# Pairs of heads, value products turned round, and the feed-forward part dealt out between score tiles: a rewrite of a hash-attention kernel

## The chip, the cores and the metric

The kernel runs on one core of one Trainium2 chip. The metric is the device time of one execution in microseconds (us); lower is better. A core has a matmul engine (PE, with a separate record PEld for loading its weights), a vector engine (DVE), an engine for activation functions (ACT), a general one (POOL), and queues that issue transfers (DMA). A matmul holds one operand still in the array, the weights or stationary operand, and streams the other past it column by column. In these kernels its results land in PSUM, a memory whose parts are called banks, and DVE and ACT read them there and write theirs to SBUF, where the operands lie. The "granted clock" is the share of full speed at which PE's clock ran, as the profile records it.

Times quoted are medians of several executions. The jobs ran on several chips; the old kernel's median was between 422.7 and 424.2 us in all of them. A run is labelled slow when it lies more than 1.5% above the fastest of the same kernel.

## The reference, cut to what matters

```python
# q, k, v: (4, 8, 768, 64); proj: (64, 6)
q_bits = (einsum('bhsd,dk->bhsk', q, proj) > 0)      # six sign bits for each token
k_bits = (einsum('bhsd,dk->bhsk', k, proj) > 0)
mask   = q_bucket[..., :, None] == k_bucket[..., None, :]
scores = where(mask, q @ k.T / sqrt(64), -1e9)
attn   = softmax(scores)                             # a tiny constant is added to the sum
x      = (attn @ v).transpose(0, 2, 1, 3).reshape(3072, 512)
h = x @ w_in                                         # layer 1: 512 -> 2048
return (h * cos(h)) @ w_out                          # layer 2: 2048 -> 512
```

Both kernels get the mask without a masking step: they append the six bits as ±constants to the 64 columns of q and k, so that a score is much larger where all six agree, and a bias in the exp brings every other score down to zero. The bits need fp32, because a product near zero must have the right sign. That is "the hash".

## The kernel before

It takes one head after the other, and starts the feed-forward part when all 32 heads are done. For a head, PE transposes q and k in fp32, DVE copies the result out of PSUM, PE does the hash matmul on it, DVE turns the sums into bits:

```python
def emit_prep_a(hd):                                     # L142
    for t in range(SB):                                  # SB = 6
        nc.tensor.matmul(out=psum_t[:, t*P:(t+1)*P], lhsT=qk_nat[:, t, :],
                         rhs=ident, is_transpose=True, ...)
    nc.vector.tensor_copy(out=qk_f32, in_=psum_t)
    ...
def emit_prep_b(hd):                                     # L159
    for c0, c1 in ((0, 512), (512, 768)):
        nc.tensor.matmul(out=psum_t[0:38, c0:c1], lhsT=projx2,
                         rhs=qk_f32[:, c0:c1], start=True, stop=True)
    nc.vector.tensor_scalar(out=q_ext[D:KEXT, :], in0=psum_t[0:NBITS, :], ...)   # bits of q
    nc.vector.tensor_scalar(out=k_ext[D:KEXT, :], in0=psum_t[32:32+NBITS, :], ...)
```

Then six score tiles of 128 keys by 768 queries, an exp of each, and the value products. There V (64 columns, and 64 columns of ones for the denominator) is the stationary operand and the exp tile streams, 768 columns and one more:

```python
out_ps = att_ps.tile([P, 1024], FP32, name="out_ps")     # two banks, one buffer
def emit_attnv(jt):                                      # L210
    for ci, (c0, c1) in enumerate(((0, 512), (512, S + 1))):
        nc.tensor.matmul(out=out_ps[:, c0:c1], lhsT=v_ext[:, jt, :],
                         rhs=pt_sb[:, c0:c1], start=(jt == 0), stop=(jt == SB - 1))
...
nc.vector.tensor_scalar(out=numpair[b][t][r0:r0+D, :], in0=out_ps[0:D, 0:S], ...)
nc.scalar.copy(out=denpair[b][t][r0:r0+D, :], in_=out_ps[D:P, 0:S])   # on ACT
```

When all heads are done, ACT computes 1/den as exp(−ln(den)), DVE multiplies, and six chunks of 512 tokens go through layer 1 and then layer 2.

The softmax here doesn't subtract the row's maximum and nothing guards it: scores larger than these inputs give would overflow.

Of the kernel before, what the change touches and what calls it, by code (L numbers as in the profile page):

```python
# [11 lines left out]
FP16 = mybir.dt.float16  # L12

Q_PRESCALE = 1.0 / 416.0
EXP_SCALE = 52.0
EXP_BIAS = -78.0
# [4 lines left out]
def kernel(  # L21
# [11 lines left out]

# [5 lines left out]
    N_TOK = B * S  # L39
    P = 128  # L40
    SB = S // P
    KEXT = D + NBITS
    NH = B * H
    NFT = D_MODEL // P
    NFF = D_FF // P

    glob = ctx.enter_context(tc.tile_pool(name="glob", bufs=1))

    ident = glob.tile([P, P], FP32)
    make_identity(nc, ident)  # L50

    projx2 = glob.tile([P, 38], FP32)
    nc.vector.memset(projx2, 0.0)
    nc.sync.dma_start(out=projx2[0:D, 0:NBITS], in_=proj)
    nc.sync.dma_start(out=projx2[D:2 * D, 32:32 + NBITS], in_=proj)

    exp_bias = glob.tile([P, 1], FP32)
    nc.vector.memset(exp_bias, EXP_BIAS)
    cos_bias = glob.tile([P, 1], FP32)
    nc.vector.memset(cos_bias, math.pi / 2.0)  # L60

    v_ext_bufs = []
    for i in range(3):
        vt = glob.tile([P, SB, P], FP16, name=f"v_ext{i}")
        nc.vector.memset(vt[:, :, D:P], 1.0)
        v_ext_bufs.append(vt)



    win_t = [glob.tile([P, D_FF], FP16, name=f"win{ft}") for ft in range(NFT)]  # L70
    wout_t = [glob.tile([P, D_MODEL], FP16, name=f"wout{ff}") for ff in range(NFF)]

    xT = [glob.tile([P, N_TOK], FP16, name=f"xT{i}") for i in range(NFT)]

    fence = [glob.tile([P, 1], FP32, name=f"fence{i}") for i in range(4)]

    stage_pool = ctx.enter_context(tc.tile_pool(name="stage", bufs=1))
    numpair = [[stage_pool.tile([P, S], FP32, name=f"num{bb}_{t}") for t in range(NFT)]
               for bb in range(B)]
    denpair = [[stage_pool.tile([P, S], FP32, name=f"den{bb}_{t}") for t in range(NFT)]  # L80
               for bb in range(B)]

    def emit_weight_loads(which):
        if which == 0:
            for ft in range(NFT):
                nc.gpsimd.dma_start(
                    out=win_t[ft], in_=moe_w_in[ft * P:(ft + 1) * P, :]
                )
        else:
            for ff in range(NFF):  # L90
                nc.gpsimd.dma_start(
                    out=wout_t[ff], in_=moe_w_out[ff * P:(ff + 1) * P, :]
                )

    att_stack = ExitStack()
    att_nat = att_stack.enter_context(tc.tile_pool(name="att_nat", bufs=3))
    att_f32 = att_stack.enter_context(tc.tile_pool(name="att_f32", bufs=2))
    att_ops = att_stack.enter_context(tc.tile_pool(name="att_ops", bufs=2))
    att_vs = att_stack.enter_context(tc.tile_pool(name="att_vs", bufs=2))
    att_ptp = att_stack.enter_context(tc.tile_pool(name="att_pt", bufs=1))  # L100
    att_ps = att_stack.enter_context(tc.tile_pool(name="att_ps", bufs=1, space=bass.MemoryType.PSUM))
    att_ps2 = att_stack.enter_context(tc.tile_pool(name="att_ps2", bufs=2, space=bass.MemoryType.PSUM))

    NPT = 6
    pt_bufs = []
    for i in range(NPT):
        ptb = att_ptp.tile([P, S + 8], FP16, name=f"pt_buf{i}")
        nc.vector.memset(ptb[:, S:S + 8], 1.0)
        pt_bufs.append(ptb)

    dma_state = {}
    prep_state = {}

    def emit_dma_v(hd):
        b, h = divmod(hd, H)
        v_ext = v_ext_bufs[hd % 3]
        nc.gpsimd.dma_start(
            out=v_ext[:, :, 0:D],
            in_=v[b, h].rearrange("(t p) d -> p t d", p=P),
        )  # L120

    def emit_dma(hd, k_engine=None, defer_v=False):
        b, h = divmod(hd, H)
        qk_nat = att_nat.tile([P, SB, 2 * D], FP32, name="qk_nat")
        nc.sync.dma_start(
            out=qk_nat[:, :, 0:D],
            in_=q[b, h].rearrange("(t p) d -> p t d", p=P),
        )
        (k_engine or nc.sync).dma_start(
            out=qk_nat[:, :, D:2 * D],  # L130
            in_=k[b, h].rearrange("(t p) d -> p t d", p=P),
        )
        v_ext = v_ext_bufs[hd % 3]
        if not defer_v:
            emit_dma_v(hd)
        dma_state[hd] = (qk_nat, v_ext)

    def emit_prep_a(hd):
        qk_nat, v_ext = dma_state.pop(hd)
        psum_t = att_ps.tile([P, SB * P], FP32, name="psum_t", space=bass.MemoryType.PSUM)  # L140
        for t in range(SB):
            nc.tensor.matmul(  # L142
                out=psum_t[:, t * P:(t + 1) * P],
                lhsT=qk_nat[:, t, :],
                rhs=ident,
                is_transpose=True,
                start=t in (0, 4),
                stop=t in (3, 5),
            )
        qk_f32 = att_f32.tile([P, S], FP32, name="qk_f32")  # L150
        nc.vector.tensor_copy(out=qk_f32, in_=psum_t)
        q_ext = att_ops.tile([KEXT, S], BF16, name="q_ext")
        k_ext = att_ops.tile([KEXT, S], BF16, name="k_ext")
        prep_state[hd] = [psum_t, qk_f32, v_ext, q_ext, k_ext]

    def emit_prep_b(hd):
        psum_t, qk_f32, v_ext, q_ext, k_ext = prep_state[hd]
        for c0, c1 in ((0, 512), (512, 768)):
            nc.tensor.matmul(  # L159
                out=psum_t[0:38, c0:c1],  # L160
                lhsT=projx2,
                rhs=qk_f32[:, c0:c1],
                start=True,
                stop=True,
            )
        nc.vector.tensor_scalar(  # L166
            out=q_ext[D:KEXT, :],
            in0=psum_t[0:NBITS, :],
            scalar1=0.0,
            scalar2=0.5,  # L170
            op0=mybir.AluOpType.is_gt,
            op1=mybir.AluOpType.subtract,
        )
        nc.vector.tensor_scalar(  # L174
            out=k_ext[D:KEXT, :],
            in0=psum_t[32:32 + NBITS, :],
            scalar1=0.0,
            scalar2=0.5,
            op0=mybir.AluOpType.is_gt,
            op1=mybir.AluOpType.subtract,  # L180
        )

    def emit_prep_c(hd):
        psum_t, qk_f32, v_ext, q_ext, k_ext = prep_state[hd]
        nc.vector.tensor_scalar(
            out=q_ext[0:D, :], in0=qk_f32[0:D, :], scalar1=Q_PRESCALE,
            scalar2=None, op0=mybir.AluOpType.mult,
        )
        nc.vector.tensor_copy(out=k_ext[0:D, :], in_=qk_f32[D:2 * D, :])

    emit_dma(0, k_engine=nc.scalar)
    emit_dma(1, k_engine=nc.scalar, defer_v=True)
    emit_prep_a(0)
    emit_prep_c(0)
    emit_prep_b(0)
    emit_dma(2, k_engine=nc.scalar, defer_v=True)
    emit_prep_a(1)
    emit_dma_v(1)

    for hd in range(NH):  # L200
        b, h = divmod(hd, H)
        _psum_t, _qk_f32, v_ext, q_ext, k_ext = prep_state.pop(hd)

        out_ps = att_ps.tile([P, 1024], FP32, name="out_ps", space=bass.MemoryType.PSUM)
        pt_tiles = {}

        def emit_attnv(jt):
            pt_sb = pt_tiles.pop(jt)
            for ci, (c0, c1) in enumerate(((0, 512), (512, S + 1))):
                nc.tensor.matmul(  # L210
                    out=out_ps[:, c0:c1],
                    lhsT=v_ext[:, jt, :],
                    rhs=pt_sb[:, c0:c1],
                    start=(jt == 0),
                    stop=(jt == SB - 1),
                )

        for jt in range(SB):
            st_ps = att_ps2.tile([P, S], FP32, name="st_ps", space=bass.MemoryType.PSUM)
            for c0, c1 in ((0, 512), (512, 768)):  # L220
                nc.tensor.matmul(  # L221
                    out=st_ps[:, c0:c1],
                    lhsT=k_ext[:, jt * P:(jt + 1) * P],
                    rhs=q_ext[:, c0:c1],
                    start=True,
                    stop=True,
                )
            pt_sb = pt_bufs[(hd * SB + jt) % NPT]
            nc.scalar.activation(  # L229
                out=pt_sb[:, 0:S],  # L230
                in_=st_ps,
                func=mybir.ActivationFunctionType.Exp,
                bias=exp_bias,
                scale=EXP_SCALE,
            )
# [13 lines left out]
        if hd + 3 < NH:  # L249
            emit_dma(hd + 3)  # L250
# [175 lines left out]
```

## Time and profile before

| | before |
|---|---|
| time, median of three (range) | 423.73 us (423.16 to 424.43) |
| profiled span, mean granted clock | 420.9 us, 0.983 |
| attention (first exp to last head) | 225.6 us, 7.08 us a head |
| change-over with PE nearly idle | 10.0 us |
| feed-forward part but for its tail | 154.0 us, PE without a gap |

The prediction below shows most of the views that this table is from. Two readings are added here. The first is the timeline of ACT in the middle of attention: start, length, engine, line, operation, result and source, how many; in brackets, the idle time ahead of it and what ended that.

```profile
121.93 0.90 ACT L229 ACTIVATE pt_buf_161<-st_ps,exp_bias 128x768 f16<-128x768 f32 x1 [1.07 <-PE st_ps L221]
122.73 0.89 ACT L229 ACTIVATE pt_buf_163<-st_ps,exp_bias 128x768 f16<-128x768 f32 x1
123.65 0.80 ACT L271 COPY den_3_131<-out_ps 64x768 f32<-64x768 f32 x1
124.47 0.90 ACT L229 ACTIVATE pt_buf_165<-st_ps,exp_bias 128x768 f16<-128x768 f32 x1
```

The COPY is that of the denominator out of `out_ps`. Successive exps start 0.80 us apart though each is recorded at 0.90.

The second is one wait of PE from the list of waits (engine, result, line, whom it waits for: us in total, times, longest).

```profile
PE h_ps L321 <- DVE xT_97 L304: 8.3, 1, 8.3
```

This is the change-over: the first layer-1 matmul waits for the normalised x.

### The profile page before, as it was taken

What the parts mean: (1) busy time and instruction counts of PE and PEld (TensorE: products, weight loads), DVE (VectorE), ACT (ScalarE), POOL (GpSimd) and SP (SyncE); (2) the same over time, 40 slices, a digit from 0 to 9 for tenths busy, and PEclk for the clock granted to TensorE, in tenths of its full rate; (3) what the DMA queues carried; (4) which work ended last, traced back from release to release, by engine and by line L of the source; (5) the groups of instructions that cost most, each with busy time, mean ns of one, the idle gap of its engine ahead of it and who ended that gap; (6) DMA issues with size and microseconds to landing.
All of it is one profiled execution on the core that took longest, in us unless ns stands there. A gap on an engine that the chain in (4) does not pass through costs nothing.

```text
span 420.9 us, 5065 instructions
## 1 busy us (share of the span) xinstructions
PE 384.4 (91%) x1856; PEld 176.4 (42%) x1856; DVE 243.1 (58%) x352; ACT 306.9 (73%) x389; POOL 37.9 (9%) x58
## 2 busy tenths in 40 slices
PE   4889999999999999999999739999999999999996
PEld 1334444444444444444343314444444444444442
DVE  3576676767686768676867337348355372360630
ACT  1478787878787878787878998968788781660831
POOL 6260101010101010111100000000000000000000
PEclk9899999999999999999999959999999999999999
DMA  9999363636363636363611000020020110200202
GB/s 171 206 198 180 62 81 57 83 55 87 52 90 50 93 47 95 48 94 48 93 11 9 0 2 1 0 101 0 0 101 1 51 51 0 101 0 2 100 25 75
DMA packets 81784, 26.54 MB, mean 63 GB/s; under 512 B 76128, under 2 KB 78176, under 8 KB 81760
## 3 DMA queue, kind: packets, MB, share of 16 engines
q1 hardware_dynamic: 51440, 18.29, 18.6%
q0 software_dynamic: 27968, 7.34, 17.1%
q10 hardware_dynamic: 2352, 0.59, 0.7%
q8 instruction: 14, 0.23, 0.2%
q14 instruction: 10, 0.08, 0.1%
HBM read 27.27 MB, written 6.29 MB: 80 GB/s over the span
## 4 chain that ended last, share of the span: by engine, by line
PE 71%; ACT 18%; DVE 5%; issue 4%; DMA 1%; ACTq 0%
PE h_ps L321 20%; PE out_ps L210 10%; PE st_ps L221 9%; PE psum_t L159 8%; ACT pt_buf_167 L229 6%; PE psum_t L142 5%; ACT pt_buf_165 L229 3%; ACT pt_buf_163 L229 3%; ACT pt_buf_161 L229 1%; DMA qk_nat<-in_k_dram 1%; PE o_ps_3374 L353 1%; PE o_ps_3149 L364 1%; PE o_ps_3147 L364 1%; PE o_ps_2925 L364 1%; PE o_ps_2923 L364 1%
## 5 line engine op out<-in xcount | busy, mean ns | idle before, releaser
L337 DVE TENSOR_TENSOR g_sb<-h_ps,cos_sb 128x512 f16<-128x512 f32 x96 | 65.3, 691 | 58.5 <-ACT cos_sb L329 58.3
L221 PE MATMUL st_ps<-q_ext,k_ext 70*128 70x512 bf16 (+1 forms) x384 | 94.2, 328 | 3.6 <-ACT pt_buf_161 L229 1.0
L329 ACT ACTIVATE cos_sb<-h_ps,cos_bias 128x512 f16<-128x512 f32 x96 | 64.8, 692 | 13.9 <-PE h_ps L321 13.4
L221 PEld LDWEIGHTS <-k_ext 70*128 70x128 bf16 x384 | 34.5, 97 | 63.7 <-issue 46.9
L229 ACT ACTIVATE pt_buf_161<-st_ps,exp_bias 128x768 f16<-128x768 f32 x32 | 28.8, 901 | 41.9 <-PE st_ps L221 41.9
L364 PEld LDWEIGHTS <-g_sb 128*128 128x128 f16 x320 | 31.2, 98 | 37.8
L321 PE MATMUL h_ps<-xT_97,win_77 128*128 128x512 f16 x96 | 36.9, 386 | 8.3 <-DVE xT_97 L304 8.3
L142 PE MATMUL psum_t<-ident,qk_nat 128*128 128x128 f32 x192 | 36.5, 277 | 6.8 <-DMA qk_nat<-in_k_dram 4.8
L255 DVE TENSOR_SCALAR vsum_sb<-out_ps 128x1 f32<-128x1 f32 x32 | 5.1, 158 | 62.8 <-PE out_ps L210 62.8
L321 PE MATMUL h_ps<-xT_98,win_78 128*128 128x512 f16 x96 | 36.8, 385 | 0.0
L321 PE MATMUL h_ps<-xT_99,win_79 128*128 128x512 f16 x96 | 36.6, 384 | 0.0
L321 PE MATMUL h_ps<-xT_100,win_80 128*128 128x512 f16 x96 | 36.6, 384 | 0.0
L166 DVE TENSOR_SCALAR q_ext<-psum_t 6x768 bf16<-6x768 f32 x32 | 30.4, 949 | 5.3 <-PE psum_t L159 4.3
L142 PEld LDWEIGHTS psum_t<-ident,qk_nat 128*128 128x128 f32 x192 | 24.1, 142 | 18.5 <-issue 7.6
L229 ACT ACTIVATE pt_buf_165<-st_ps,exp_bias 128x768 f16<-128x768 f32 x32 | 28.8, 901 | 3.4 <-PE st_ps L221 2.7
L229 ACT ACTIVATE pt_buf_167<-st_ps,exp_bias 128x768 f16<-128x768 f32 x32 | 28.8, 901 | 3.1 <-PE st_ps L221 0.7
L174 DVE TENSOR_SCALAR k_ext<-psum_t 6x768 bf16<-6x768 f32 x32 | 30.5, 952 | 0.4
L229 ACT ACTIVATE pt_buf_171<-st_ps,exp_bias 128x768 f16<-128x768 f32 x32 | 28.9, 902 | 0.0
L229 ACT ACTIVATE pt_buf_163<-st_ps,exp_bias 128x768 f16<-128x768 f32 x32 | 28.6, 893 | 0.0
L229 ACT ACTIVATE pt_buf_169<-st_ps,exp_bias 128x768 f16<-128x768 f32 x32 | 28.6, 893 | 0.0
L321 PEld LDWEIGHTS <-win_77 128*128 128x128 f16 x96 | 9.5, 99 | 19.9 <-issue 8.8
L210 PEld LDWEIGHTS <-v_ext_73 128*128 128x128 f16 x132 | 12.8, 97 | 7.7 <-issue 1.7
(721 smaller groups left out, 603.1 us busy)
## 6 DMA issues: line engine op xcount, KB each, us to landing
qk_nat<-in_q_dram SPq DMA_DIRECT2D x32, 192.0 KB, 2.8
out_dram<-o_sb SPq DMA_DIRECT2D x24, 256.0 KB, 2.0
qk_nat<-in_k_dram SPq DMA_DIRECT2D x29, 192.0 KB, 3.9
v_ext_71<-in_v_dram POOLq DMA_DIRECT2D x11, 96.0 KB, 4.6
v_ext_73<-in_v_dram POOLq DMA_DIRECT2D x11, 96.0 KB, 4.3
v_ext_75<-in_v_dram POOLq DMA_DIRECT2D x10, 96.0 KB, 4.3
qk_nat<-in_k_dram ACTq DMA_DIRECT2D x3, 192.0 KB, 4.9
win_77<-in_moe_w_in_dram POOLq DMA_DIRECT2D x1, 512.0 KB, 8.9
```

Of the source, the lines that this page charges most:

```text
L142: nc.tensor.matmul(out=psum_t[:, t * P:(t + 1) * P], lhsT=qk_nat[:, t, :], rhs=ident, is_transpose=True, start=t in (0, 4), stop=t in (3, 5),)
L159: nc.tensor.matmul(out=psum_t[0:38, c0:c1], lhsT=projx2, rhs=qk_f32[:, c0:c1], start=True, stop=True,)
L166: nc.vector.tensor_scalar(out=q_ext[D:KEXT, :], in0=psum_t[0:NBITS, :], scalar1=0.0, scalar2=0.5, op0=mybir.AluOpType.is_gt, op1=mybir.Alu ...
L174: nc.vector.tensor_scalar(out=k_ext[D:KEXT, :], in0=psum_t[32:32 + NBITS, :], scalar1=0.0, scalar2=0.5, op0=mybir.AluOpType.is_gt, op1=myb ...
L210: nc.tensor.matmul(out=out_ps[:, c0:c1], lhsT=v_ext[:, jt, :], rhs=pt_sb[:, c0:c1], start=(jt == 0), stop=(jt == SB - 1),)
L221: nc.tensor.matmul(out=st_ps[:, c0:c1], lhsT=k_ext[:, jt * P:(jt + 1) * P], rhs=q_ext[:, c0:c1], start=True, stop=True,)
L229: nc.scalar.activation(out=pt_sb[:, 0:S], in_=st_ps, func=mybir.ActivationFunctionType.Exp, bias=exp_bias, scale=EXP_SCALE,)
L255: nc.vector.tensor_scalar(out=vsum_sb[:, 0:1], in0=out_ps[:, S:S + 1], scalar1=DELTA, scalar2=None, op0=mybir.AluOpType.mult,)
L321: nc.tensor.matmul(out=h_ps, lhsT=win_t[ft][:, ff * P:(ff + 1) * P], rhs=xT[ft][:, tok0:tok0 + TOK_CHUNK], start=(ft == 0), stop=(ft == NF ...
L329: nc.scalar.activation(out=cos_sb, in_=h_ps, func=mybir.ActivationFunctionType.Sin, bias=cos_bias, scale=1.0,)
L337: nc.vector.tensor_tensor(out=g_sb, in0=h_ps, in1=cos_sb, op=mybir.AluOpType.mult)
L364: nc.tensor.matmul(out=o_ps[tt], lhsT=g_tiles[ff][:, tt * P:(tt + 1) * P], rhs=wout_t[ff], start=(ff == 0), stop=(ff == NFF - 1),)
```

## The change

Its author describes it as "preparation of the first pairs in single steps on units of their own; whole-pair hash at once; value products skipped there and doubled between". Against the kernel before it is a complete rewrite. A "pair" is two heads, a "unit" is one score tile with its exp; there are 192 units. The parts that matter are these, as cut excerpts from both sides.

The value products change their stationary operand. A head's result then needs 396 columns (461 with the small constant in columns of its own), one bank, so two heads can alternate:

```diff
-    for ci, (c0, c1) in enumerate(((0, 512), (512, S + 1))):
-        nc.tensor.matmul(
-            out=out_ps[:, c0:c1],
-            lhsT=v_ext[:, jt, :],
-            rhs=pt_sb[:, c0:c1], ...
+    bank = av_ps[h % 2]
+    for qt in range(T):                                    # T = 6
+        nc.tensor.matmul(
+            out=bank[:, qt * W:qt * W + D + 1],
+            lhsT=pt[:, qt * P:(qt + 1) * P],               # the exp tile is stationary
+            rhs=vx_bufs[pr % 3][:, hh, jt, 0:D + 1], ...   # 65 columns stream
```

The hash of a pair is eight fp32 matmuls of 192 columns. Each of four (q or k, head) goes to 32 columns of the array of its own:

```diff
-    nc.tensor.matmul(out=psum_t[0:38, c0:c1], lhsT=projx2, rhs=qk_f32[:, c0:c1], ...
+    for c in range(2):
+        for j, (w, hh, ts) in enumerate(cols):
+            nc.tensor.matmul(
+                out=hb[32 * j:32 * j + 32, :].rearrange("p (t r) -> p t r", r=32),
+                lhsT=projblk[:, c].rearrange("p b i -> p (b i)"),
+                rhs=blk[pr][w][:, hh, ts[0]:ts[-1] + 1, c, :],
+                start=(c == 0), stop=(c == 1), ...
```

Its input `blk` comes from DVE block transposes. For pairs 0 to 4 small PE matmuls and fp16 PE transposes bring bits and operands into place; for pairs 5 to 15 it is DMA transposes and, for the bits, a DMA. The normalisation is a reciprocal and a multiply on DVE for each head (from the ninth head on after a small copy and an add), and after the start ACT has no copies left. Last, the schedule. Layer 2 of a batch is dealt out among the units of the next, and the steps for pairs 1 to 4 are spread over units, most with one of its own, on which value products are skipped unless more than three units of them are pending:

```diff
+    UF = lambda u: 2 if u % 2==0 else 1        # layer-2 matmuls for a unit
+    ENDF = 6
+    PREP = {1: [0.5, 2, 4.5, 6, 7.5, 9, 9.5, 12, 14], ...}
+    HEAVY = set(int(x) for n in PREP for x in PREP[n][3:]) | set(int(x) for x in SECOND)
...
+        for u in range(U):
+            score(h, jt)
...
+            elif u in HEAVY:
+                avs = len(pend) - MAXP
+            else:
+                avs = min(2, len(pend) - (4 if u < T else LAG))
+            for _ in range(avs):
+                av_step()
...
+            if b > 0:
+                fill(UF(u))                    # layer 2 of the batch before
```

## The prediction

> **What bounds the kernel now.** I read the page first, then the busy time by stage, then the longest pieces of the chain of waits, then single instructions by shape. The page says that the matmul engine is nearly always busy and carries most of the chain; busy is not peak, so the stages have to be told apart.
>
> ```profile
> PE 384.4 (91%) x1856; PEld 176.4 (42%) x1856; DVE 243.1 (58%) x352; ACT 306.9 (73%) x389; POOL 37.9 (9%) x58
> ...
> PE 71%; ACT 18%; DVE 5%; issue 4%; DMA 1%; ACTq 0%
> ```
>
> Busy time in five stretches: up to the first exp, the attention, the change-over, the feed-forward part, its last chunk. The first column after the stretch is its length, then come PE, weight loads, DVE, ACT, POOL, clock, DMA share, GB/s.
>
> ```profile
> 0.00:13.36 13.36, 5.50 (x19) 2.72 (x20) 5.64 (x18) 1.28 (x1) 7.55 (x17) 1.00 1.14 179
> 13.36:239.00 225.64, 209.68 (x1065) 97.77 (x1064) 156.16 (x217) 185.86 (x222) 30.32 (x41) 0.99 0.54 79
> 239.00:249.00 10.00, 1.37 (x8) 0.56 (x7) 2.39 (x5) 9.90 (x12) 0.00 (x0) 0.69 0.00 0
> 249.00:403.00 154.00, 154.00 (x705) 69.25 (x705) 77.59 (x113) 106.78 (x151) 0.00 (x0) 0.99 0.09 35
> ```
>
> The feed-forward stretch has no PE idle time at all; attention is 93% busy; the change-over of 10 us is Ln and Exp on ACT with PE waiting (8.3 us in the chain). Unit prices, from the chain and the groups by shape:
>
> ```profile
> 403.07 3.45 PE o_ps_3371 L353 x16
> ...
> L221 PE MATMUL st_ps<-q_ext,k_ext 70*128 70x512 bf16 x192 | 71.9, 383 | 3.6 <-ACT pt_buf_161 L229 1.0 <-ACT pt_buf_165 L229 0.3 <-ACT pt_buf_163 L229 0.3
> L221 PE MATMUL st_ps<-q_ext,k_ext 70*128 70x256 bf16 x192 | 52.2, 272 | 0.0
> ...
> L142 PE MATMUL psum_t<-ident,qk_nat 128*128 128x128 f32 x192 | 36.5, 277 | 6.8 <-DMA qk_nat<-in_k_dram 4.8 <-issue 2.1
> ```
>
> Sixteen 512-column matmuls take 3.45 us, 0.216 us each, though a single one is recorded at 383 ns: overlap. The 256-column form follows its predecessor by 0.11 us (383 minus 272 ns says the same). So a score tile of 512+256 columns costs 0.325 us of PE. An fp32 hash matmul of 512 columns shows as two records that together last 1.05 us (four passes), and the fp32 transposes start 0.108 us apart. One head takes 7.08 us (its starts are 121.43, 128.51, 135.59), in which streaming is 1.95 scores + 1.95 value products + 1.28 hash + 0.65 transposes = 5.83; the remaining 1.25 us is PE waiting behind the serial chain transposes, DVE copy, hash, DVE bits. Over the kernel: 32 x 1.25 = 40 us of such holes, 13 us start, 8 us change-over, 4 us tail; streaming itself is 62 + 62 + 41 + 21 + 83 + 83 = 352 us.
>
> **What the Trainium skill says.** "TensorE: Matmul & The Clock Gate", section "Back-to-back issue gap": N/2.4 + 2.5 ns for a warm matmul; 0.216 us at 512 columns agrees. The same section gives about 81 ns for 128-column matmuls that each have their own weight load; the old kernel has no small fp16 matmul, so no trace shows it. Its Part 3, "Packing small matmuls", says that matmuls into different 32-column strips run together; not shown yet either. "FP8 and Floating Point Precision", section "TensorE Precision Notes", puts true fp32 at four passes; the 1.05 us above agree. "ScalarE: Activation LUTs", section "Step-by-step: what each stage is for", tells of about 2.7 us for a table load including the drain; here the record is 1.283 us.
>
> **The change part by part.** It is a rewrite. The order of instructions in both builds gives the counts.
>
> 1. Feed-forward arithmetic is the same: layer 1 is 512 matmuls of 384 columns at 0.1625 (estimate from the page's formula), 83.2 us; layer 2 is 384 x 0.216 = 82.9 us. What is new is that layer 2 of one batch is dealt out, one and two matmuls in turn, among the score tiles of the next batch, so that PE has work while ACT does exp.
> 2. Scores: 192 x 0.325 = 62.4 us, unchanged. Exp: 192 x 0.79 (the spacing of successive exps in the timeline) = 152 us of ACT. Exp of batch 0 alone is 56 x 0.79 = 44 us.
> 3. Value products turn round: the exp tile becomes the weight, 65 columns of V stream. 1152 pairs of weight load and matmul replace 384 long matmuls (62.4 us). Price per pair between 0.030 (65/2.4 + 2.5 ns, load hidden) and 0.081 (the page's figure for 128 columns). I choose 0.047: 54 us. This is the largest unknown.
> 4. The 192 fp32 transposes (21 us) go. In their place: DVE 32x32 transposes for the hash, 120 fp16 PE transposes for pairs 0 to 4 (0.07 each, estimate, 8.4 us), DMA transposes for the other eleven pairs.
> 5. Hash: 8 fp32 matmuls of 192 columns per pair, 1536 columns x 4 passes, 2.56 us alone, to four column strips in turn. I take two at a time: 1.5 us a pair, 24 us against 41. Bits of pairs 0 to 4: 24 small matmuls a pair at 0.05 (estimate), 6 us together.
> 6. Normalisation becomes a reciprocal and a multiply on DVE per head; the 32 denominator copies (0.80 us each) and 32 Ln/Exp activations (about 0.85 each) leave ACT, and with them the change-over. x is turned by 16 DMA transposes.
>
> By stage, with 0.325 + 6 x 0.047 = 0.607 per unit: first score at 9 us (13 minus the fp32 hash and transpose of a whole head). Units 0 to 55: 34.0 + four pairs of 4.4 (hash 1.5, bits 1.2, transposes 1.7) + 3.5 for the second half of pair 0 and the delta matmuls = 55 (above ACT's 44). Layer 1 of batch 0: 128 x 0.1625 + one table load 1.3 = 22.1. Batches 1 and 2: 48 x (0.607 + 1.5 x 0.216) = 44.7 + four hashes 6 = 50.7 each, 101.4. Their layer 1 with 16 fills: 25.6 each, 51.2. Batch 3: 40 x 0.931 + 4.5 = 41.7. Left-over value products and layer 2: 4. Layer 1 and 2 of batch 3: 20.8 + 20.7. Last copy and store: 3. Sum 329. The measured time exceeds the profiled span by 2.8 (423.7 against 420.9); 3 more for waits that I did not see: **335 us**. Attention and its change-over give all of it, 249 us to about 165 us of PE time; the feed-forward part gives nothing by itself.
>
> **The rivals.**
> - *The small matmuls cost the page's 81 ns.* 1152 x 0.034 more = 39 us, and some for bits and transposes: 380 us. For it: the weight load, 97 ns in the trace, must be paid somewhere when only 27 ns of streaming hide it. Against: the 97 ns are mostly latency, for loads of 128 fp32 columns hide behind matmuls 0.108 us apart.
> - *The load hides fully and ACT becomes the bound.* At 0.030 the units lose 0.10 us each, some 20 us. A unit is then 0.83 us of PE with its share of hash 0.95, just above exp's 0.79, so ACT limits only batch 0: 317 to 320 us.
> - *The hash does not overlap between strips*: 16 us more, 350. *It overlaps four-wide*: 10 us less.
> - *A new wait*: DVE in batch 0 (copies of 768 fp16 columns out of PSUM, estimate 0.9 us each from the 0.96 us of the old copy, four a pair, plus block transposes) is about 7.5 us of 12 units' 11 us, so close that a late copy stalls a score; POOL now does casts for which no trace has a price; the DMA transposes have five units (about 5 us) to land. Each could add 5 to 15 us, against which speaks that the steps are spread out on units of their own.
>
> **Range and chances.** The price of a small pair moves the sum between 318 and 380, the hash between 325 and 350. I hold 0.03 for about one in three, 0.04 to 0.06 for one in two, 0.08 for one in six. Hence 335, with 313 to 366 eight times in ten. Even with every rival against it the time stays under 415, so slower is left only for a stall I can't see: faster 0.97, within 2% 0.02, slower 0.01.
>
> **What would show it.** Right: no gap of PE over 1 us between the first score and the last tile; line of the value products at 0.04 to 0.06 us start to start; layer 1 at 0.163 and layer 2 at 0.216; exp gaps on ACT in batches 1 to 3, almost none in batch 0; first exp near 9 us; clock 1.0 throughout. Wrong: PE waiting for DVE copies or a DMA transpose at each pair, or value products at 0.08. The prediction fails most likely through the price of the small pairs, next through batch 0.

## The result, and the profile after

| | before | after |
|---|---|---|
| median of four runs of one job (range) | 423.71 us (423.16 to 424.43) | 311.23 us (310.70 to 312.90) |
| ratio (95% interval) | | 0.7356 (0.7333 to 0.7378) |
| profiled span, clock | 420.9 us, 0.983 | 309.5 us, 0.998 |

A ratio here and below is the mean time of one kernel's fast runs over the mean of the other's fast runs in the same rounds, so it is not quite the ratio of the medians. The kernel gained 112.5 us, and 311.23 lies 1.8 us below the predicted range.

The page of the changed kernel: busy time, share of the span and count for each engine, and who carries the chain that ended last.

```profile
PE 299.1 (97%) x3026; PEld 180.2 (58%) x3026; DVE 201.2 (65%) x434; ACT 234.6 (76%) x288; POOL 109.2 (35%) x180
...
PE 79%; ACT 7%; DMA 6%; DVE 4%; issue 2%; POOL 1%; SPq 0%; ACTq 0%; DVEq 0%
```

PE's share rose from 91% to 97% while its busy time fell by 85 us, and ACT's part of the chain fell from 18% to 7%. Next, the busy time in ten stretches of the changed kernel, all but its tail of 3.2 us; the columns are those of the prediction's table (length, PE, weight loads, DVE, ACT, POOL, clock, DMA share, GB/s).

```profile
0.00:8.59 8.59, 6.74 (x65) 2.80 (x66) 3.19 (x14) 2.90 (x6) 3.67 (x18) 1.00 0.67 199
8.59:57.39 48.80, 45.96 (x768) 31.80 (x767) 32.48 (x78) 45.68 (x56) 34.65 (x50) 1.00 0.80 204
57.39:80.20 22.81, 22.68 (x148) 13.59 (x148) 16.55 (x26) 17.88 (x24) 13.27 (x34) 1.00 0.89 164
80.20:124.00 43.80, 42.65 (x507) 26.07 (x506) 35.37 (x88) 39.77 (x48) 27.69 (x39) 1.00 0.77 180
124.00:150.00 26.00, 26.00 (x171) 15.23 (x170) 18.15 (x27) 17.92 (x25) 2.67 (x4) 1.00 0.18 60
150.00:195.00 45.00, 43.75 (x511) 26.45 (x510) 34.70 (x90) 41.02 (x49) 23.97 (x33) 1.00 0.74 164
195.00:221.00 26.00, 26.00 (x171) 15.23 (x170) 17.38 (x26) 17.91 (x24) 0.43 (x1) 1.00 0.04 13
221.00:264.70 43.70, 43.70 (x458) 25.70 (x457) 23.19 (x61) 36.33 (x43) 2.90 (x4) 1.00 0.31 76
264.70:285.50 20.80, 20.80 (x130) 12.53 (x128) 14.26 (x21) 14.29 (x20) 0.00 (x0) 1.00 0.04 13
285.50:306.30 20.80, 20.79 (x113) 10.77 (x110) 5.50 (x8) 0.90 (x1) 0.00 (x0) 1.00 0.19 69
```

In the first stretch with exps (8.59 to 57.39) ACT is busy for 45.7 of 48.8 us: exp is the bound there. In every later one shown PE is, with at most 1.25 us free. These stretches set against the prediction's sum:

| stage | predicted, us | measured, us |
|---|---|---|
| up to the first exp | 9 | 8.6 |
| units 0 to 55 | 55 | 48.8 |
| layer 1 of batch 0 | 22.1 | 22.8 |
| units of batch 1; its layer 1 | 50.7; 25.6 | 43.8; 26.0 |
| units of batch 2; its layer 1 | 50.7; 25.6 | 45.0; 26.0 |
| units of batch 3 and left-overs | 45.7 | 43.7 |
| layer 1, layer 2 of batch 3, tail | 20.8 + 20.7 + 3 | 20.8 + 20.8 + 3.2 |
| sum | 329 | 309.5 |

What one unit looks like, in PE's timeline:

```profile
100.09 0.48 PE L257 MATMUL s_ps<-qx,kx 128*128 128x512 f16 x2
100.41 0.34 PE L283 MATMUL av_ps<-vx,pt 128*128 128x65 f16 x6
100.59 0.59 PE L375 MATMUL m_ps<-wout,g 128*128 128x512 f16 x2
```

From the start of the six value products (100.41) to the start of what follows (100.59) is 0.18 us, 0.03 us for each, although the groups of the same kernel by line (busy us, mean ns of one) say 97 ns for a weight load and 193 for its matmul:

```profile
L283 PEld LDWEIGHTS <-pt 128*128 128x128 f16 x1152 | 56.9, 97 | 19.9 <-issue 0.4
...
L283 PE MATMUL av_ps<-vx,pt 128*128 128x65 f16 x1152 | 64.0, 193 | 0.0
```

Both are latencies that overlap with their neighbours. Only start-to-start spacing is a price. Taken over the whole trace, that spacing is 29 ns for a value pair (median), 0.81 us for the hash of a pair of heads and 0.30 us for a pair's bits (means of pairs 1 to 15 and 1 to 4), and 56 ns for an fp16 transpose (median).

Where PE's time went, as the sum of the intervals from each matmul record to the next, by purpose (a wait is counted to the matmul before it, so the change-over of 8.3 us sits under the value products of the kernel before):

| purpose | before, us | after, us |
|---|---|---|
| layers 1 and 2 | 167.6 | 169.4 |
| scores | 86.5 | 64.8 |
| value products | 79.1 | 42.2 |
| hash, bits, transposes | 78.6 | 23.6 |
| warm-up matmuls | 0 | 5.2 |
| sum | 411.8 | 305.2 |

The feed-forward work cost the same. The gain is in attention: hash and transposes 55 us, value products with the change-over 37 us, and 22 us of waits behind the scores.

### The profile page after: what moved, and what is told of

It reads as the page before. It is cut to its first block, busy times and chain, and to the rows that moved or that the text cites. A ratio compares the mean times of both kernels' runs of the same rounds, so it can differ in the third digit from the quotient of the medians.

```text
span 309.5 us, 7586 instructions
## 1 busy us (share of the span) xinstructions
PE 299.1 (97%) x3026; PEld 180.2 (58%) x3026; DVE 201.2 (65%) x434; ACT 234.6 (76%) x288; POOL 109.2 (35%) x180
## 3 DMA queue, kind: packets, MB, share of 16 engines
q0 software_dynamic: 6576, 17.17, 20.8%
## 4 chain that ended last, share of the span: by engine, by line
PE 79%; ACT 7%; DMA 6%; DVE 4%; issue 2%; POOL 1%; SPq 0%; ACTq 0%; DVEq 0%
PE m_ps L375 23%; PE s_ps L325 18%; PE s_ps L257 16%; PE av_ps L283 8%; ACT pt L263 7%; PE m_ps L325 6%; DMA kx<-br 3%; PE m_ps L169 3%; DMA natk<-in_k_dram 2%; PE av_ps L325 2%; PE m_ps L359 1%; PE m_ps L229 1%; DVE kx L248 1%; DVE blkq L156 1%; DVE g L342 1%
## 5 line engine op out<-in xcount | busy, mean ns | idle before, releaser
L263 ACT ACTIVATE pt<-s_ps,exp_bias 128x768 f16<-128x768 f32 x192 | 162.0, 899 | 12.9 <-PE s_ps L257 11.1
L375 PE MATMUL m_ps<-wout,g 128*128 128x512 f16 x368 | 105.6, 379 | 0.1
L257 PE MATMUL s_ps<-qx,kx 128*128 128x512 f16 (+1 forms) x384 | 93.7, 326 | 4.9 <-ACT pt L263 2.0
L325 PEld LDWEIGHTS <-win 128*128 128x128 f16 x512 | 50.0, 98 | 34.5 <-issue 0.2
L283 PEld LDWEIGHTS <-pt 128*128 128x128 f16 x1152 | 56.9, 97 | 19.9 <-issue 0.4
L283 PE MATMUL av_ps<-vx,pt 128*128 128x65 f16 x1152 | 64.0, 193 | 0.0
L325 PE MATMUL s_ps<-xT,win 128*128 128x384 f16 x352 | 62.3, 326 | 0.1
L342 DVE TENSOR_TENSOR g<-s_ps,cos 128x768 f16<-128x768 f32 x44 | 42.1, 958 | 28.1 <-ACT cos L337 28.1
L337 ACT ACTIVATE cos<-s_ps,cos_bias 128x768 f16<-128x768 f32 x44 | 39.7, 902 | 26.8 <-PE s_ps L325 25.4
L257 PEld LDWEIGHTS <-kx 128*128 128x128 f16 x384 | 34.8, 97 | 34.8 <-issue 5.3
```

The costliest lines, as they stand in the source:

```text
L257: nc.tensor.matmul(out=sp[:, c, 0:c1 - c0], lhsT=kx(pr)[:, hh, jt * P:(jt + 1) * P], rhs=qx(pr)[:, hh, c0:c1], start=True, stop=True)
L263: nc.scalar.activation(out=pt, in_=sp.rearrange("p c n -> p (c n)")[:, 0:S], func=ACTF.Exp, bias=exp_bias, scale=EXP_SCALE)
L283: nc.tensor.matmul(out=bank[:, qt * W:qt * W + D + 1], lhsT=pt[:, qt * P:(qt + 1) * P], rhs=vx_bufs[pr % 3][:, hh, jt, 0:D + 1], start=Fal ...
L325: nc.tensor.matmul(out=halves[c][:, 0:C2], lhsT=win_t[ft][:, ff * P:(ff + 1) * P], rhs=xT[(b, ft)][:, 3 * c:3 * c + 3, :], start=(ft == 0) ...
L337: nc.scalar.activation(out=c_, in_=h_, func=ACTF.Sin, bias=cos_bias, scale=1.0)
L342: nc.vector.tensor_tensor(out=g_, in0=h_, in1=c_, op=ALU.mult)
```

## The experiments

Most expectations name theories of their own, A and B. All kernels give the reference's result unless it is said that one is wrong. "More" and "less" are against the changed kernel's 311.23 us, which was measured in another job; the kernel before ran in every job, and the ratio to it is the comparison within one job.

### What a value pair costs

**Twice the value products.** Each pair is issued twice; numerator and denominator double, the result stays the same.

```diff
+            for again in range(2):
                 nc.tensor.matmul(
                     out=bank[:, qt * W:qt * W + D + 1],
-                    start=False, stop=(jt == T - 1 and qt == T - 1), ...
+                    start=False, stop=(jt == T - 1 and qt == T - 1 and again == 1), ...
```

> Changed kernel with every value product (weight load and 65-column matmul) issued twice; result stays right because numerator and denominator double together. Theory A, a pair costs its start-to-start spacing of 0.029 us and PE is the bound from batch 1 on: 136 units x 6 x 0.029 = 23.7 us more there, and in batch 0, where ACT is the bound, between 3 and 9 us: 338 to 345 us. Rival B, the load is only cheap because the bursts are short, six pairs, and twelve in a row expose it (0.05 us or more a pair): 360 us or more. Rival C, PE is not the bound of the units: under 325 us.

Measured: 339.41 us (338.51 to 339.72), ratio 0.8014. The 28.2 us above the changed kernel are 24.5 ns for each of 1152 more pairs; the spacing says 29. In its trace the time up to layer 1 of batch 0 grew by 6.5 us for 336 more pairs (19 ns each), where PE has time to spare, and the rest by 21.5 us for 816 (26 ns). The small price is confirmed by time, not only by the trace.

**Half the columns.** 33 of the 65 columns stream, with the same weight loads (wrong).

> Changed kernel with only columns 32 to 64 of V streamed, 33 instead of 65 (wrong result on purpose). If streaming sets the pair[...], the spacing falls to 16 to 25 ns and the time by 4 to 12 us, to 299 to 307. If the weight load sets it, the spacing stays at 0.029 us and the time at 311.

Measured: 307.0 us (306.85 to 307.99), ratio 0.7256. The spacing fell from 29 to 25 ns and not to 16. So at 65 columns the streaming counts, and just below it there is a floor; whether the floor is that of the matmul or of the load with it, this run does not show.

**A control and a slower load.** The control adds the small constant by one wide matmul for every head rather than for the first eight (`DPE = B * H`), so that the next kernel can use 126 weight columns.

> Control for the next run: the delta term of all heads by a 390-column matmul, as in batch 0, in place of a 65-column one and a DVE add. 24 x (0.167 - 0.029) = 3.3 us more of PE, 24 x 0.78 us less of DVE. If PE is the bound: 314 to 315. If DVE were: below 311.

Measured: 312.96 us (311.60 to 313.25), ratio 0.7386: nearly as before, a little less than expected. Then, on top of it, 126 of the 128 weight columns (wrong; the fast load that the expectation names is explained below it):

```diff
-                out=bank[:, qt * W:qt * W + D + 1],
-                lhsT=pt[:, qt * P:(qt + 1) * P],
+                out=bank[0:P - 2, qt * W:qt * W + D + 1],
+                lhsT=pt[:, qt * P:(qt + 1) * P - 2],
```

> The control with exp-tile weights of 126 columns instead of 128 (two rows of 128 wrong on purpose)[...]. Theory A, the pairs are cheap because of that fast load:[...] pairs at 0.053 us or more, 1152 x 0.024 = 28 us, less some slack in batch 0: 335 to 345 us. Rival B, any load is hidden by being pulled ahead: no change from the control, 314 to 315.

Measured: 335.22 us (334.38 to 336.22), ratio 0.7912, 22 us above the control. PE's timeline of a unit:

```profile
101.11 0.48 PE L283 MATMUL av_ps<-vx,pt 128*126 128x65 f16 x6
101.42 0.60 PE L375 MATMUL m_ps<-wout,g 128*128 128x512 f16 x2
```

and the load's group by line:

```profile
L283 PEld LDWEIGHTS <-pt 128*126 128x126 f16 x1152 | 90.0, 137 | 18.3
```

Six pairs now take 0.31 us in place of 0.18; the median spacing is 57 ns. A load recorded at 137 rather than 97 ns no longer hides. The Trainium skill, "TensorE: Matmul & The Clock Gate", section "Weight-path perf modes", says that a fast weight load is used when the number of weights is 128 and the type is not fp32; this run agrees. So a value pair is cheap because its tile is exactly 128 wide (widths other than 126 and 128 were not run).

### What the hash costs

**Another order of issue.** The loops over `c` and over the strips `j` are exchanged, so that two matmuls of one strip follow each other.

> Changed kernel with the two loops around the hash matmul exchanged, so that the four records into one 32-column strip follow each other instead of going to four strips in turn; same arithmetic, right result. Theory A, four strips at once make a pair's hash cost 0.92 us instead of 16 x 0.163 = 2.6: the new order overlaps only at the three strip changes, 2.1 to 2.2 us a pair, 11 pairs x 1.25 = 14 us plus 2 to 5 in batch 0: 325 to 331 us. Rival B, 32-column matmuls are cheap by themselves: 311.

Measured: 311.25 us (309.87 to 311.57), ratio 0.7339: nothing. In the trace four records of alternating source still start within 40 ns, and the next four 0.16 us later, although they were issued two to a strip, so the engine seems to run a strip ahead of another's unfinished work. The order of issue was therefore no test of parallelism.

**All on one strip.** For pairs 1 to 15 all four write to the first 32 columns (wrong).

```diff
-                    out=hb[32 * j:32 * j + 32, :].rearrange("p (t r) -> p t r", r=32),
+                    out=(hb[0:32, :] if pr else hb[32 * j:32 * j + 32, :]).rearrange("p (t r) -> p t r", r=32),
-                    start=(c == 0), stop=(c == 1),
+                    start=(c == 0 or pr > 0), stop=(c == 1 or pr > 0),
```

> Changed kernel with the hash matmuls of pairs 1 to 15 all written to the first 32-column strip (wrong result on purpose). Theory A, four strips in parallel make the hash cheap: 16 records x 0.163 = 2.6 us a pair instead of 0.92, 11 pairs x 1.7 = 19 us and 2 to 6 in batch 0: 330 to 337 us. Rival B, small matmuls are cheap by themselves: 311.

Measured: 338.27 us (337.94 to 339.33), ratio 0.7998, 27 us more. The spacing is 162 ns, and the intervals of all hash matmuls sum to 42.5 us against 13.8. DVE's wait for the sums, by line (busy us, mean ns, idle before and what ended it), first in the changed kernel:

```profile
L177 DVE TENSOR_SCALAR bh<-m_ps 128x192 f16<-128x192 f32 x15 | 5.4, 357 | 7.8 <-PE m_ps L169 7.8
```

and with one strip:

```profile
L177 DVE TENSOR_SCALAR bh<-m_ps 128x192 f16<-128x192 f32 x15 | 5.4, 358 | 36.0 <-PE m_ps L169 36.0
```

PE's hash intervals grew by 28.7 us and DVE's wait by 28.2, beside 27 us of time. This edit also makes all four write one place in PSUM, so alone it does not tell strips from places; the records do the rest: in the changed kernel those of the four strips start some 7 ns apart and the next four about 0.16 us later, with one strip single records start 0.162 us apart. That the four strips run at once is shown; the prediction had taken two.

### What the schedule is worth

**Layer 2 as a block.** No fills between units, 96 matmuls after each layer 1 (`UF = lambda u: 0`, `ENDF = 96`).

> Changed kernel with layer 2 of a batch in one block behind its layer 1 and nothing filled between the score tiles; same arithmetic, right result. Theory A: units then need 0.57 us of PE and run at the pace of exp, 0.79 to 0.80; each of three batches takes 38 us plus a block of 20.7 that no exp covers instead of 44 to 45 plus 4.8 of fills elsewhere: about 10 to 12 us more each, 340 to 348 us. Rival B, the interleaving only moves PE work and PE was the bound anyway: within 5 us of 311.

Measured: 351.81 us (351.01 to 352.53), ratio 0.8308, 41 us more and a little above what was expected. Two stretches of this kernel, columns as above: the layer-2 block, then units of batch 1.

```profile
80.00:102.00 22.00, 21.94 (x121) 10.12 (x120) 5.34 (x9) 2.69 (x4) 3.92 (x6) 1.00 0.36 123
102.00:140.00 38.00, 31.36 (x410) 20.66 (x410) 31.45 (x82) 35.65 (x45) 24.23 (x34) 1.00 0.74 162
```

In the block ACT is busy for 2.7 of 22 us, and in the units that follow it is the bound (35.65 of 38.00) while PE has 6.6 us of holes. Each engine rests while the other works. This is the largest of the parts that I took out alone.

**No skipping of value products.** `HEAVY = set()`.

> Changed kernel without the rule that units with preparation steps skip value products and later ones double them. Theory A, batch 0 is bound by exp (44.2 of its 48.8 us), and the rule keeps ACT fed: 1 to 4 us more in batch 0, 312 to 315. Rival B, the rule does nothing for the time: 311 within 0.5.

Measured: 311.79 us (310.85 to 312.43), ratio 0.7356. No effect can be measured, though the change names this part in its title.

**Preparation in one lump.** Hash, bits and transposes of each of pairs 1 to 4 all on one unit.

```diff
-                units = PREP[n]
+                units = PREP[n][:3] + [PREP[n][5]] * 6
```

> Changed kernel with hash, bits and the four transposes with their copies of pairs 1 to 4 all on one unit instead of six. Theory A: PE waits for DVE five times in a row in that unit (bits 0.36 + 0.31, copies 0.55 each), 3 to 4 us a pair of which exp in flight hides about 1.5: 5 to 12 us more, 316 to 323. Rival B, the order in time doesn't matter since PE has slack in batch 0: within 2 us.

Measured: 323.69 us (323.48 to 324.76), ratio 0.7644, 12.5 us more. ACT's timeline shows where:

```profile
22.04 9.63 ACT L263 ACTIVATE pt<-s_ps,exp_bias 128x768 f16<-128x768 f32 x12 [3.74 <-PE s_ps L257]
...
35.29 4.86 ACT L263 ACTIVATE pt<-s_ps,exp_bias 128x768 f16<-128x768 f32 x6 [3.62 <-PE s_ps L257]
```

One gap of 3.6 to 4.0 us for each of the four pairs, while PE and DVE do the chain hash, bits, transposes, copies with no score between. Single steps are thus worth 12.5 us; skipping the value products beside them adds nothing.

**One bank for the value products.** `av_ps[1]` for every head.

> Changed kernel with one bank for all value products instead of two in turn; right result. Theory, the second bank lets value products of a head start while DVE still reads the head before: each of 32 heads then waits about 1.0 to 1.5 us (copy 0.21, add 0.57, or reciprocal and multiply, after the last product) of which units in flight hide part: 325 to 350 us. Rival, PE has enough other work queued behind: under 315.

Measured: 325.0 us (323.28 to 326.52), ratio 0.7659, 14 us more. PE waits here for DVE to empty the bank, 20 times:

```profile
PE av_ps L278 <- DVE tot L306: 8.0, 20, 0.5
```

In batch 0 it waits another 3.3 us, 4 times, for the normalising multiply. A second result buffer is worth 14 us to a kernel whose PE is otherwise full. The turned-round product is what makes room for it.

### What bounded the head of the kernel before

**The kernel before without its hash matmuls** (wrong: the two `projx2` matmuls go, the rest stays).

> Kernel before without its hash matmuls (wrong result on purpose; the DVE bit steps stay). Theory A: a head falls from 7.08 us to the 5.9 that ACT needs for it (5.87 busy), because with PE relieved ACT is the next bound: 32 x 1.15 = 37 us less and some 4 at the start, 382 to 390 us. So a cheaper hash alone could give less than half of the 112 us. Rival B, the whole 1.28 of streaming plus 1.25 of holes goes: 32 x 2.5 = 80 us less, 343 us.

Measured: median 432.37 us; the one fast run 425.8 us, three others 432.2 to 434.9 labelled slow. Neither expectation came true: even the fast run is no faster than the kernel before in the same job (median 422.72), though 1.28 us of matmul a head is gone. The profiled run was a slow one, so I take no size from it. It does show the granted clock falling to half inside attention, which the fast run shares in part (mean clock 0.967 against 0.98 to 0.99 of the kernel before). Two stretches of it, columns as above:

```profile
74.91:78.32 3.41, 2.20 (x11) 1.06 (x11) 3.33 (x5) 3.36 (x5) 0.00 (x0) 1.00 0.98 144
78.32:81.74 3.42, 3.42 (x15) 2.15 (x13) 0.64 (x1) 2.00 (x3) 0.00 (x0) 0.50 0.00 0
```

PE was busy for 2.20 of 3.41 us before the clock of 0.50, and its longest single gap in this part of attention was 0.72 us. Where the clock is full, a head of this kernel takes 6.99 us in the mean against 7.08, so the hash alone is worth some 3 us (estimate, 32 x 0.09), and the falling clock took more than that back.

So something else holds a head at 7 us. The timeline of ACT above suggested what: the denominator copy is queued behind two exps of the next head, and until it ends, the next head's value products have nowhere to go, as there is one `out_ps`. Hence two more kernels, both wrong. **Without the denominator copy** (POOL fills the tile with a constant instead):

```diff
-        nc.scalar.copy(out=denpair[b][t][r0:r0 + D, :], in_=out_ps[D:P, 0:S])
+        nc.gpsimd.memset(denpair[b][t][r0:r0 + D, :], 16.0)
```

> Kernel before with the ACT copy of the denominators (0.80 us a head) replaced by a POOL fill (wrong result on purpose). If the chain through the one value-product tile sets a head's 7.08 us, it falls by 0.4 to 1.0 us a head, 391 to 410 us. If PE sets it, as the prediction says, nothing changes: 420 to 424.

Measured: 422.81 us (422.09 to 423.42), ratio 0.9991: the same. **Without both hash and copy:**

> Kernel before without hash matmuls and without the denominator copy (wrong result on purpose). If the chain is the bound and the hash only fills its holes: about the time of the run without the copy alone, or somewhat more where the clock falls in idle windows. If PE is the bound once the chain is shorter: 15 us or more below that run.

Measured: 398.91 us (397.85 to 399.74), ratio 0.9434. One stretch of attention in each of three kernels, columns as above. The kernel before:

```profile
100.00:160.00 60.00, 55.88 (x286) 25.78 (x285) 43.45 (x61) 49.62 (x60) 7.40 (x9) 1.00 0.51 73
```

Without the copy:

```profile
100.00:160.00 60.00, 55.88 (x289) 26.30 (x287) 42.36 (x59) 42.94 (x52) 7.38 (x9) 1.00 0.48 69
```

Without both:

```profile
100.00:160.00 60.00, 52.89 (x289) 27.93 (x288) 48.83 (x67) 47.11 (x59) 7.40 (x9) 1.00 0.57 80
```

Taking the copy away frees 6.7 us of ACT in 60 and moves nothing, PE's busy time included. A head takes 7.07 us without the copy and 6.89 or 7.10, in turn, without the hash where the clock is full, but 6.22 or 6.35 without both: 0.8 us a head, 32 x 0.8 = 25 us. PE's waits from 100 us on show one limit in each kernel (total us, times, longest). Without the copy PE still waits for the DVE copy on the way to the hash, once a head:

```profile
PE psum_t L159 <- DVE qk_f L151: 7.6, 19, 0.4
```

Without the hash it waits, once a head, for the denominator copy, besides waits for exps:

```profile
PE out_ps L202 <- ACT den L263: 6.3, 19, 0.3
```

Without both, the two are gone from the list and only waits for exps are left inside attention. The old head had two limits of nearly equal length: the hash (its matmuls and the chain through it, which these runs do not separate) and the chain through the single `out_ps` with the copy on ACT. Removing the second alone gives nothing, the first alone next to nothing. The rewrite removes both.

### The transfers of later pairs

PE's timeline of the changed kernel has one gap longer than 1 us between units:

```profile
118.22 0.50 PE L257 MATMUL s_ps<-qx,kx 128*128 128x512 f16 x2 [1.15 <-DMA kx<-br]
```

A score waits for the transfer that brings the bits of k. **Copy of k and transfer of all bits two units earlier** (pairs 7 to 15; step 7 becomes 5):

> Changed kernel with copy and bit transfers of pairs 7 to 15 two units (1.8 us) earlier. Theory A: the stalls of PE for these transfers at 117 and 178 us (1.2 us each) go: 308.5 to 309.5. Rival B, the copies then hold up DVE or wait for the DMA transposes: 311 or more.

Measured: 321.55 us median (316.63 to 323.41); the three fast runs, 316.63 to 320.37, give a ratio of 0.754. Worse even in the fast runs. The waits (total us, times, longest) of the profiled execution, which was a slow one:

```profile
PE s_ps L325 <- DMA xT<-xn: 9.9, 2, 8.3
```

PE no longer waits for bits of k, but layer 1 waits for the transfers that turn x. DVE now waits 21.1 us, in 14 pieces, for the DMA transposes that deliver k. That this holds up DVE's other work and the transfers behind it is my reading, from one execution. The control below was not in this job, but the kernel before ran at its usual 422.72 us in it. **Bits of k only**, two units after the hash, while the copy and the bits of q stay:

```diff
-                    bits_dma(n, (0, 1, 2, 3))
-                steps = [start, hsh, hsh2, kc]
+                    bits_dma(n, (0, 2))
+                def kb(n=n):
+                    bits_dma(n, (1, 3))
+                steps = [start, hsh, hsh2, kc, kb]
...
+                units = units + [units[2] + 2]
```

> Changed kernel with the bit transfers of the keys issued two units after the hash, before the key copy, instead of after it; right result. Theory: two of the four issues (0.7 us each) leave the end of the chain, stalls of PE for bits (1.2 us at two places) go: 308.5 to 310. Rival: the SP queue waits for the shuffles and holds up the DMA transposes behind it: 311 or more.

Measured: 309.21 us (308.75 to 309.77), ratio 0.7284 (0.7241 to 0.7328). The changed kernel itself, in the same job as a control:

> The changed kernel unedited, beside the next two on one chip. 310 to 313 us if the chip makes no difference; 318 or more if the slow results of the early bits and of the missing POOL sums came from the chip.

Measured: 310.95 us (310.59 to 312.59), ratio 0.7336 (0.7295 to 0.7377). The intervals overlap, but none of the four runs of one lies among the four of the other, and the wait for the bits of k is gone from the list. It is some 0.6% better, and the fastest kernel that gives the right result.

**POOL without its sums.** In the changed kernel DVE's normalising multiply takes longer while POOL works. Two entries of DVE's timeline; at the first POOL was adding (0.99 us from 108.46), at the second it rested but for the first 0.06 us:

```profile
108.72 1.15 DVE L310 TENSOR_TENSOR xn<-tot,rc 128x384 f16<-128x384 f32 x1
...
174.71 0.56 DVE L310 TENSOR_TENSOR xn<-tot,rc 128x384 f16<-128x384 f32 x1
```

The Trainium skill, "SBUF — State Buffer", section "SBUF: two separate sides", says that a DVE instruction with two SBUF inputs and a POOL instruction that reads SBUF exclude each other. These two entries agree, and so does the add of line 306, which takes one input from PSUM and stays at 565 ns in the mean. The experiment replaces POOL's three additions by a copy (wrong), twice, the second time beside the control:

```diff
-        half = vsp.tile([P, 2, 3, D], FP32, name="vhalf")
-        nc.gpsimd.tensor_tensor(out=half, in0=nv[:, :, 0:3, :], in1=nv[:, :, 3:6, :], op=ALU.add)
...
+        nc.gpsimd.tensor_copy(out=vs_bufs[pr % 3][:, :, 0:D], in_=nv[:, :, 0, :])
```

> Changed kernel with the three POOL adds per pair that sum V replaced by one small copy (delta term wrong on purpose). Theory A: the DVE multiply at L310, 0.56 us when POOL rests and 1.15 when POOL adds two tensors, gets shorter (mean 0.83 to about 0.6), but DVE is not the bound, so the time stays at 310 to 311.5. Rival B: DVE latency is on the path of units: 2 us or more less.

> The kernel without POOL sums once more. If the edit makes it slow (loads issued earlier collide with bit transfers): 323 to 331 us beside 311 for the control. If it was the chip: 310 to 312.

Measured: 327.14 us (325.56 to 331.02; the highest labelled slow), ratio 0.7767, and 329.95 us (326.90 to 331.54), ratio 0.7768. The multiply did fall, from 834 to 558 and 584 ns in the mean, but the kernel lost 16 to 19 us. In the second of the two runs PE waits for transfers:

```profile
PE s_ps L252 <- DMA kx<-br: 10.7, 6, 2.9
```

In the changed kernel this wait is 1.7 us in total. Layer 1 waits another 4.2 us, once, for a transfer of x; in the changed kernel it does not. POOL, with less to do, issues the loads of later pairs 1.0 us after it begins to cast v rather than 3.0 us (in both runs, against both traces of the changed kernel), and they take longer to land (v 8.5 and 8.6 us against 5.8 and 5.5). That earlier loads collide with the transposes and bits transfers is my reading; no run shows why, and it stays open.

## Why the prediction was right and wrong

**Right: the mechanism and the direction.** Attention and its change-over gave the gain, the feed-forward part gave nothing, PE became the bound of everything after batch 0, and layer 1 and layer 2 cost 0.1625 and 0.216 us a matmul as it said. Most of its marks held: first exp at 8.59 us, clock 0.998, exp gaps on ACT after batch 0. Two did not: one stall of PE was over 1 us (1.15), and the value products were below 0.04 us.

**Wrong: the price of a value pair.** This is the step that failed: "I choose 0.047: 54 us". It measured 0.029, which takes 1152 x 0.018 = 20.7 us off the sum. The prediction had this price in hand as its lower bound (0.030, load hidden) and gave it one chance in three, because it let a page's 81 ns for 128 columns pull the middle up. The trace of the kernel before had said more: fp32 loads recorded at 142 ns in the mean belong to transposes that start every 108 ns, so the recorded length is no cost. The run with double products shows by time that the small price is real, and the run with 126 columns that a pair costs 57 ns when its load is not the fast one; 0.047 was between the two and is neither.

**Wrong: the hash, two strips at a time.** 1.5 us a pair was taken, 0.81 measured, 15 x 0.69 = 10.4 us. The run on one strip shows four at once.

**Wrong: bits and transposes.** 0.30 us a pair in place of 1.2 (4 x 0.9 = 3.6 us; these matmuls go to strips too) and 0.056 in place of 0.07 each (1.4 us).

**Errors of the other sign hid nearly half of this.** With the four measured prices the sum would be 329 − 36.1 = 292.9, and 309.5 was measured. The missing 16.6 us are: units 0 to 55, where PE's corrected sum of 41 us falls below ACT's 44.2 and 48.8 was measured, +7.6; batch 3 and its left-overs, +4.4, most of it because 30 layer-2 matmuls were left over (96 less 6 less 40 x 1.5) where the 4 us had room for half as many; batch 2, +2.3, and batch 1, +1.1, with the waits for bits of k among them; the layer-1 stages, +1.5; start and end −0.2. Beyond the sum, the prediction added 2.8 us for the time outside the profiled span and 3 for unseen waits; 1.7 was measured (311.23 less 309.5), another 4.1 us too much. So "55 (above ACT's 44)" failed as a reading of the bound, once PE was cheaper: the prediction said itself, under its second rival, that ACT limits batch 0 then.

**Wrong: the range took the rivals one by one.** The hidden load alone was said to give 317 to 320 us, four strips alone 10 less. Both came true, and together they lie below the low end of 313.

**Partly wrong: what held a head of the kernel before.** "The remaining 1.25 us is PE waiting behind the serial chain transposes, DVE copy, hash, DVE bits" names one of two limits. Without the denominator copy nothing was gained, without the hash some 3 us by estimate, and without both 25 us. It made no error in the sum, as the rewrite removes both, but it would have misled anyone who wished to mend the old kernel with one edit. One small reading of the prediction is turned round, without harm: a score's 256-column matmul starts 0.215 us after the 512-column one, and what follows it 0.108 us later; the 0.325 stands.

**The feared new waits.** Late DVE copies in batch 0 did not stall the changed kernel; the lumped version shows that they would have, for 12.5 us, without single steps. The DMA transposes landed in time, and the transfers of bits cost a stall of 1.15 us.

## What to carry to other kernels

Price small matmuls by start-to-start spacing, not by recorded length: with a weight tile of exactly 128 columns and a type of 16 bits the load was free here even under 65 streamed columns, and that makes it pay to keep the wide operand still and stream the narrow one. If a stage shows holes on PE, look for every chain that is as long as the stage before removing one, since of two nearly equal limits neither alone gave more than some 3 us here. Where one engine is the bound of one stage and another of the next, deal the second stage's work out among the first (41 us here), and when giving a range, let favourable rivals come true together.

## What the Trainium skill lacked or had wrong

- "TensorE: Matmul & The Clock Gate", "Back-to-back issue gap", calls 81 ns at 128 columns and 131 ns at 512 the sustained spacing of pairs of load and matmul. The runs show 56 ns at 128 columns, 29 at 65 and 216 at 512, all with a load for each. Its formula for a single matmul (N/2.4 + 2.5 ns) fits all three; its floor of about 25 ns agrees with the run of 33 columns.
- The same page, "LDWEIGHTS", puts a load at the number of columns over 1.2, which is 105 ns for 126 columns. The run with 126 columns was recorded at 137 ns and cost 57 ns a pair; with 128 columns it cost nothing above streaming. So neither figure of this run is 105, and the section has no price for such a load in a stream of pairs. That a fast load is about twice as fast is stated on the page under "Weight-path perf modes", and 57 against 29 ns a pair agrees.
- The same page, Part 3, "What overlaps and what doesn't", calls matmuls strictly first in, first out. With the hash issued two to a strip, records of four strips still started within 40 ns of each other. That is read from the records alone.
- The same page, "HAM oscillation", speaks of idle gaps of over 3.4 us. In the kernel before without its hash the granted clock fell to 0.50 after a stretch with PE busy for 2.20 of 3.41 us, with no gap above 0.72 us. In that execution, one of the slow ones, the clock fell eight times inside attention; cut into stretches of 3.41 us in step with these falls, PE was busy for 1.92 to 2.33 us in the stretch before each, and for 2.30 us or more in every stretch at full clock that no fall followed. The page's next section tells of short idle times that let the clock fall, but has no share of busy time.
